# Forward and backward of a speech joint network on one core: fe rows by a transposing transfer, the first chunk's h in another tile, fewer ge loads, longer landing margins

## The chip, the cores and the metric

The kernel runs on one core of a Trainium2 chip. The metric is the device time of one execution in microseconds; lower is better. Five engines work side by side, each through its own queue in the order in which its instructions stand: TensorE (PE, its weight loads PEld), VectorE (DVE), ScalarE (ACT), GpSimd (POOL) and SyncE (SP). Here SP only issues transfers, almost all of the kernel's; they run on 16 DMA engines.

## The reference

```python
h = sum(einsum("btc,cd->btd", xp[:, i:i+T], w1[i]) for i in range(3))     # B=2, T=16000, D=256
h = gelu(h)[:, ::2]
f = sum(einsum("btc,cd->btd", hp[:, i:i+T1], w2[i]) for i in range(3))
f = gelu(f)[:, ::2]                                                       # 2 x 4000 positions
fe = einsum("btd,de->bte", f, w_f)
ge = einsum("bud,de->bue", g, w_g)                                        # U = 8
j = tanh(fe[:, :, None, :] + ge[:, None, :, :])
out = einsum("btud,dv->btuv", j, w_o)                                     # 2 x 4000 x 8 x 256
```

The kernel returns `out` and the gradients of all seven inputs for a given `grad_out`, in bf16.

## The kernel before

The 8000 positions (both batches, after the two strides of 2) are cut into 17 chunks: one of 256 positions, fifteen of 512 (four blocks of 128), one of 64. One chunk crosses from batch 0 to batch 1 (`c.mid`). Each loop step k records three stages of different chunks, so that they overlap:

- `stage_a(k+1)`: both convolutions with their gelus and gelu derivatives, then fe. `XC` is x transposed (channels on partitions), `HT` holds h (odd and even positions) and f, `FE` is fe with channels on partitions. `fe_rows` (L573) makes `FER`, fe with positions on partitions, by eight TensorE transposes (L582) into PSUM and one evacuation (`evac`, L322 on ACT or L327 on DVE). `tile_rows` (L492) makes `HR`, the rows of h and f, by one transposing transfer on SP.
- `stage_j(k)`: four steps of two u each. `JT` = tanh(fe + ge) with channels on partitions (ACT, L637); `JR`, the same with positions on partitions, from `FER` plus `GEB` (ge broadcast to all partitions) added on DVE (L660) and tanh on ACT (L665). The first two chunks (k < `NTR` = 2) have no `FER` and transpose `JT` on TensorE instead (L655). `GO_R` and `GOT` are `grad_out` as loaded and transposed. Products: `out` from JT and WO, grad w_o (`GWO`) from JR and GO_R, grad j from GOT and WOT, times 1 - tanh squared (L696, L705), summed over u into `GN` (L720).
- `stage_de(k-1)`: back through w_f, w2, w1 (`GN`, `GH` with channels on partitions), their rows `GNR` and `GHR` by transposing transfers (`grad_rows`, L759), weight gradients from HR, GNR, GHR and `XR` (rows of x), grad x through `GX_SB`.

`load_geb` (L607) loads ge's broadcast rows from DRAM (`GED`) into `GEB`, at chunk 2, at the crossing chunk and at the one after.

The order of every queue is not the order of the code. Each operation is recorded with its engine choices, an estimated cost, what it reads and writes, buffer classes with a few slots each ("ht" 1, "gh" 1, "fer" 2, "got" 3, "xc" 1 and so on), and a due time (`F.now`). `Flow.issue` (L105) then simulates the engines with these estimates and emits, one after another, the operation that can start first, with due times deciding between equals. For a transfer the model has a time to issue, a time on the one DMA ring, and a landing margin `land` after it; whoever reads the tile counts as ready only then. `ring` (L101) gives the time on the ring. So a change of `land` moves instructions on all engines without changing any of them. Nearly all matmuls are recorded through `mm` (L313), all transfers through `dma` (L337 transposing, L339 plain).

Of the kernel before, what the change touches and what calls it, by code (L numbers as in the profile page):

```python
# [35 lines left out]
class Flow:  # L36
# [5 lines left out]
    BACKLOG = {"T": 1450.0, "L": 4500.0, "S": 4500.0}  # L42
    NEAR = 300.0
    COLD = 14000.0
    KIND = 16.0

    def __init__(self, ctx, tc):
# [50 lines left out]
        self.ops.append(o)  # L98
        return o

    def ring(self, prev, kind, work):  # L101

        return work, self.TURN.get((prev or "") + kind, 0.0)

    def issue(self):  # L105
        T = {e: 0.0 for e in self.WAKE}
        avail = {e: [] for e in T}
        dma_free, dma_kind = 0.0, None
        left = len(self.ops)
        slots, seq = self.slots, self.seq  # L110

        def put(o):
            o.ready = max((d.done for d in o.deps if d not in o.soft), default=0.0)
            for e in o.eng:
                avail[e].append(o)

        for o in self.ops:
            if o.left == 0:
                put(o)
        while left:  # L120
            best = None
            for e, lst in avail.items():
                t, wake, cand, near = T[e], self.WAKE[e], None, []
                for o in lst:
                    s = o.ready + wake
                    for b in o.new:
                        st = seq[b.cls]
                        if not st[2] and st[1] != b.seq:
                            s = None
                            break  # L130
                        f = min((x[1] for x in slots[b.cls] if x[1] is not None), default=None)
                        if f is None:
                            s = None
                            break
                        s = max(s, f + wake)
                    if s is None:
                        continue
                    s = max(s, t)
                    k = (s, o.prio, o, e)
                    if e == "SP":  # L140
                        near.append(k)
                    if cand is None or k < cand:
                        cand = k
                if near:
                    lim = cand[0] + self.NEAR
                    cand = min((k for k in near if k[0] <= lim), key=lambda k: (
                        k[1][0] + (self.KIND if (k[2].xfer[0] == "T") != (dma_kind == "T") else 0.0), k[1][1]))
                if cand is not None and (best is None or cand[0] < best[0]):
                    best = cand
            assert best is not None, "no operation can start"  # L150
            s, _, o, e = best
            for x in o.eng:
                avail[x].remove(o)
            for b in o.new:
                free = [i for i, x in enumerate(slots[b.cls]) if x[1] is not None]
                i = min(free, key=lambda i: (slots[b.cls][i][1], i))
                b.slot, slots[b.cls][i][1] = i, None
                seq[b.cls][1] += 1
                b.t = slots[b.cls][i][0].tile(b.shape, b.dtype, name=b.name, tag=b.cls)
            T[e] = s + o.cost[o.eng.index(e)] * (1.8 if e == "PE" and s < self.COLD else 1.0)  # L160
            if o.xfer:
                kind, work, land = o.xfer
                if e == "SP":
                    work, gap = self.ring(dma_kind, kind, work)
# [44 lines left out]
def kernel(  # L209
# [20 lines left out]
    B, T, D = x.shape  # L230
# [130 lines left out]
    def load_xc(g_, at, apart=0.0):  # L361
# [4 lines left out]
        for n_, (b0, b1) in enumerate(cuts):  # L366
            dma("SP", lambda b0=b0, b1=b1: XC[:, b0:b1, :, :c.np].rearrange("p j k n -> p (j k) n"),
                lambda b0=b0, b1=b1: dram(xf, 4 * c.q0 - 1 + b0, 4 * c.nb, b1 - b0, c.np),
                r=[], w=[(XC, ("m", n_))], bytes_=(b1 - b0) * c.np * D * 2, new=[XC] if n_ == 0 else [], transpose=True, at=at + n_ * apart,
                land=2500.0 if c.first else 1500.0)  # L370
        if c.first:
            pool_zero(lambda: XC[:, 0, :, 0:1], [], [(XC, "z")], at=at)
            pool_copy(lambda: XC[:, 0, :, 1:P], lambda: XC[:, 4 * c.nb, :, 0:P - 1], 254, [(XC, ("m", 0))], [(XC, "h")], at=at)
# [5 lines left out]
    def load_go(g_, up, at, behind=()):  # L379
# [1 line left out]
        GO = buf("go", [P, NB, 2, V], BF16, "GO_R")  # L381
        src = gof[c.q0:c.q0 + c.W, 2 * up:2 * up + 2, :].rearrange("(p a) u v -> p a (u v)", a=c.nb)
        dma("SP", lambda: GO[:c.np, 0:c.nb].rearrange("p a u v -> p a (u v)"), lambda: src, r=[], w=[GO],
            bytes_=c.W * 1024, new=[GO], load=True, at=at, behind=behind)
        st[g_].setdefault("GO", {})[up] = GO

    def load_got(g_, up, at):
# [2 lines left out]
        GOT = buf("got", [P, NB, 2, KT, P], BF16, "GOT")  # L390
        got_op[g_, up] = dma("SP", lambda: GOT[:, 0:c.nb, :, :, :c.np].rearrange("p a j k n -> p (a j k) n"),
            lambda: GO[:c.np, 0:c.nb].rearrange("p a u v -> p (a u v)"),
            r=[GO], w=[GOT], bytes_=c.W * 1024, new=[GOT], transpose=True, at=at)
        st[g_].setdefault("GOT", {})[up] = GOT

    def load_xr(g_, at, behind=()):
# [11 lines left out]
                    r=[], w=[(XR, lo)], bytes_=(hi - lo) * nr * 512, load=True, at=at, behind=behind)  # L408
        else:
            dma("SP", lambda: flat(0, c.np), lambda: dram(xf, r0, 4 * c.nb, nr, c.np),  # L410
                r=[], w=[(XR, "m")], bytes_=c.np * nr * 512, new=[XR], load=True, at=at, behind=behind)
# [95 lines left out]
    def stage_a(g_, t0, dt):  # L507
# [2 lines left out]
        XC = S["XC"]  # L510
        nb, n_ = c.nb, c.np
        na = min(nb, 2)
        HT = buf("ht", [P, 3 * NB + 1, KT, P], BF16, "HT")
        oE, oF = nb + 1, 2 * nb + 1
        two = g_ == 1

# [38 lines left out]
        conv_gelu(g_, conv2, [hto + [W2]], HT, "f", oF, "G2", "g2", [P, NB, KT, P], None, [])  # L555
        pad_tail(g_, HT, "f", (oF, oF + nb))
        F.now = t0 + 0.48 * dt
        FE = S["FE"] = buf("fe", [P, KT, CW], BF16, "FE")
        for mt in range(KT):
            ps = psum()  # L560

# [1 line left out]
                for kt in range(KT):  # L563
                    mm(ps[:, :c.W], WF[:, kt, mt * P:(mt + 1) * P], HT[:, oF:oF + nb, kt, :n_], kt == 0, kt == KT - 1)
            op("PE", c_pe([c.W] * KT), mms, r=ftk + [WF], w=[ps], new=[ps] + ([FE] if mt == 0 else []))
            evac(lambda mt=mt: FE[:, mt, :c.W], lambda ps=ps: ps[:, :c.W], c.W, r=[ps], w=[(FE, mt)])
        F.now = t0 + 0.55 * dt
        if g_ >= NTR:
            fe_rows(g_)
        F.now = t0 + 0.75 * dt  # L570
        tile_rows(g_, "HR", "hr", HT, 3 * nb + 1, shape=[P, 3 * NB + 1, D], land=2500.0)

    def fe_rows(g_):  # L573
        c, S = chunks[g_], st[g_]
        nb, n_, FE = c.nb, c.np, S["FE"]
        FER = S["FER"] = buf("fer", [P, NB, D], BF16, "FER")
        ps = psum(BF16)

        def trs(e, ps=ps):
            for a in range(nb):  # L580
                for kt in range(KT):
                    nc.tensor.transpose(out=ps[:n_, (a * KT + kt) * P:(a * KT + kt + 1) * P],  # L582
                                        in_=FE[:, kt, a * n_:(a + 1) * n_], identity=ident[:])
        op("PE", c_pe([P] * (nb * KT)), trs, r=[FE, ident], w=[ps], new=[ps, FER])
        evac(lambda: FER[:n_, 0:nb].rearrange("p a d -> p (a d)"), lambda ps=ps: ps[:n_, 0:nb * D], nb * D,
             r=[ps], w=[FER], f=0.5)
# [18 lines left out]
            bytes_=8192, land=2500.0)  # L605

    def load_geb(c, at):  # L607
        t_ = lambda: GED[:]
        for up in range(UP):
            for lo, hi, b in parts_of(c):  # L610
                hi = P if hi == c.np else hi
                dma("SP", lambda up=up, lo=lo, hi=hi: GEB[lo:hi, 2 * up:2 * up + 2].rearrange("p u d -> p (u d)"),
                    lambda up=up, lo=lo, hi=hi, b=b: GED[b:b + 1, up * 512:(up + 1) * 512].to_broadcast([hi - lo, 512]),
                    r=[GED], w=[(GEB, up)], bytes_=(hi - lo) * 1024, load=True, at=at(up),
                    behind=[got_op[c.i - 1, 1]])

    def parts_of(c):

# [2 lines left out]
    def stage_j(g_, t0, dt):  # L621
# [2 lines left out]
        nb, n_, W = c.nb, c.np, c.W  # L624

        def cut(ap, lo, hi):
            return ap.rearrange("p (a n) -> p a n", a=nb)[:, :, lo:hi] if c.mid else ap

        def pair(up):
            F.now = tu = t0 + dt * up / UP  # L630
# [3 lines left out]
            for j in range(2):  # L634
                for mt in range(KT):
                    for k_, (lo, hi, b) in enumerate(parts_of(c)):
                        op("ACT", c_act((hi - lo) * nb, ptr=True), lambda e, j=j, mt=mt, lo=lo, hi=hi, b=b: nc.scalar.activation(  # L637
                            out=cut(JT[:, j, mt, :W], lo, hi), in_=cut(S["FE"][:, mt, :W], lo, hi), func=ACT.Tanh,
                            bias=GE[:, b, mt, 2 * up + j:2 * up + j + 1], scale=1.0),
                           r=[(S["FE"], mt), (GE, b)], w=[(JT, (j, mt, k_))],  # L640
                           new=[JT] if j == 0 and mt == 0 and k_ == 0 else [], at=tu - q * (1.0 - (2 * j + mt) / 4))
# [117 lines left out]
    def grad_rows(g_, name, cls, SRC, nblk, m):  # L759
        if chunks[g_].last:  # L760
            return pe_rows(g_, name, cls, SRC, 1, nblk, m)
        return tile_rows(g_, name, cls, SRC, nblk, lo=1, shape=[P, 2 * NB + (cls == "ghr"), D], land=3000.0)

    def stage():
        stage_n[0] += 1
# [271 lines left out]
    for b in range(B):  # L1037
# [4 lines left out]
    wload("POOL", WG, 0, lambda: WG[:], lambda: w_g.rearrange("(kt p) n -> p kt n", p=P), BIG + 1, 5000.0)  # L1042
    wload("POOL", WF, 0, lambda: WF[:], lambda: w_f.rearrange("(kt p) n -> p kt n", p=P), BIG + 2, 5000.0)
    wload("POOL", WO, 0, lambda: WO[:], lambda: w_o.rearrange("(kt p) n -> p kt n", p=P), BIG + 2, 5000.0)

    def turn(jobs, at):

# [106 lines left out]
```

## Time and profile before

| | us |
|---|---|
| median of three runs | 790.43 |
| lowest and highest of them | 787.97 and 793.09 |
| the profiled execution | 790.81 |
| its span (first to last instruction) | 789.0 |

| engine | busy us | share of the span |
|---|---|---|
| PE matmul | 769.4 | 98% |
| DVE | 719.7 | 91% |
| ACT | 711.8 | 90% |
| POOL | 83.2 | 11% |

The core moves 184.34 MB at a mean of 234 GB/s, nearly all on the SP queue. Of the groups that the change touches, the trace shows: 112 fe transposes of 128 columns on PE and two of the last chunk, 14 `FER` evacuations of 1028 ns on ACT, 16 loads of GEB, and transposing transfers `GOT` (68), `XC` (18), `HR` (17), `GNR` (16) and `GHR` (16), whose median times from issue to landing are 4.9, 9.6, 4.0, 4.4 and 7.7 us.

How to read it: a span is one execution on the profiler's clock. Matmul ends are modelled, so that PE's busy time covers the pipelining of one matmul under the next; start-to-start times say more than durations. DMA share is the mean busy share of the 16 DMA engines, and passes 1 where packets overlap on one engine. In the waits, a line says who waited for whom: total us, times, longest.

### The profile page before, as it was taken

To read this page: it belongs to the slowest core of one execution; us is meant where nothing else is said; L and a number is where in the kernel's file an instruction comes from. 1 tells how busy PE (TensorE), PEld (TensorE's weight loads), DVE (VectorE), ACT (ScalarE), POOL (GpSimd) and SP (SyncE) were. 2 spreads that over 40 slices of the span, in tenths; PEclk is the share of its full clock that TensorE was granted. 3 is DMA by queue.
4 is the path that set the end of the run, shared out by engine and by line. 5 is a ranking of instruction groups with operands and counts; after the bars stand their busy time and mean duration, and the time that the engine had idled before them with its cause. 6 is when DMAs were issued, how large, how long until landed. Compare 5 with 4: busy or idle time off the path is not lost.

```text
span 789.0 us, 15383 instructions
## 1 busy us (share of the span) xinstructions
PE 769.4 (98%) x5620; PEld 532.5 (67%) x5620; DVE 719.7 (91%) x1511; ACT 711.8 (90%) x1139; POOL 83.2 (11%) x225
## 2 busy tenths in 40 slices
PE   7899999999999999999999899999999999999997
PEld 5667667576676766767576576676757667677765
DVE  4899999998989999999999889989999899999874
ACT  4999999998899999999999799899999989999762
POOL 3011110100102010020100101002020010201000
PEclk9999999999999999999999999999999999999999
DMA  8999999999999999999999999999999999999673
GB/s 176 194 234 231 244 223 272 237 242 287 210 270 255 240 260 225 273 223 250 245 231 275 213 259 238 222 280 214 282 226 233 253 222 267 209 227 258 163 187 95
DMA packets 396052, 184.34 MB, mean 234 GB/s; under 512 B 320318, under 2 KB 389736, under 8 KB 394056
## 3 DMA queue, kind: packets, MB, share of 16 engines
q1 hardware_dynamic: 394920, 182.56, 99.6%
q8 instruction: 44, 0.72, 0.4%
q0 software_dynamic: 240, 0.41, 0.3%
q10 hardware_dynamic: 816, 0.39, 0.2%
q14 instruction: 32, 0.26, 0.1%
HBM read 52.99 MB, written 50.35 MB: 131 GB/s over the span
## 4 chain that ended last, share of the span: by engine, by line
PE 74%; ACT 8%; DVE 7%; DMA 7%; SPq 2%; issue 2%; DVEq 0%; ACTq 0%
PE ps L313 62%; PE GWO L313 10%; DMA GNR<-GN 4%; ACT JT L637 2%; ACT JSQ L696 2%; SPq L337 2%; DVE g_s L467 2%; DMA GHR<-GH 1%; DVE NGZ L705 1%; ACT JR L665 1%; ACT g_sq L463 1%; ACT HT L465 1%; PE psb L582 1%; ACT OUT_SB L322 1%; DVE ZS L720 1%
## 5 line engine op out<-in xcount | busy, mean ns | idle before, releaser
L637 ACT ACTIVATE JT<-FE,GE 128x512 bf16<-128x512 bf16 (+4 forms) x288 | 182.1, 691 | 0.0
L313 PE MATMUL ps<-GOT,WOT 128*128 128x512 bf16 (+2 forms) x544 | 150.4, 362 | 2.8 <-ACT JT L637 2.4
L705 DVE SCALAR_TENSOR_TENSOR NGZ<-JSQ,ps 128x512 f32<-128x512 bf16 (+3 forms) x252 | 151.2, 607 | 1.9 <-PE ps L313 1.7
L313 PE MATMUL ps<-WO,JT 128*128 128x256 bf16 (+1 forms) x1008 | 151.0, 273 | 0.4 <-DVE JR L327 0.3
L313 PEld LDWEIGHTS <-JT 128*128 128x128 bf16 (+1 forms) x1008 | 98.4, 98 | 62.6 <-issue 0.9
L322 ACT CAST OUT_SB<-ps 128x512 bf16<-128x512 f32 (+1 forms) x204 | 123.5, 612 | 17.2 <-PE ps L313 16.7
L696 ACT ACTIVATE JSQ<-JT 128x1024 bf16<-128x1024 bf16 (+2 forms) x126 | 129.6, 1028 | 9.7 <-DVE NGZ L705 7.6
L313 PE MATMUL GWO<-GO_R,JR 128*128 128x256 bf16 (+1 forms) x1008 | 131.0, 273 | 0.5 <-DVE JR L327 0.4
L665 ACT ACTIVATE JR<-JR 128x1024 bf16<-128x1024 bf16 (+1 forms) x116 | 123.7, 1070 | 8.2 <-DVE JR L660 8.2
L720 DVE TENSOR_TENSOR ZS<-ZS,NGZ 128x1024 f32<-128x1024 f32 (+2 forms) x102 | 115.3, 1130 | 0.7
L313 PEld LDWEIGHTS <-JR 128*128 128x128 bf16 (+1 forms) x1008 | 98.0, 98 | 16.6 <-DVE JR L327 0.7
L313 PEld LDWEIGHTS <-W 128*128 128x128 bf16 x636 | 61.0, 99 | 60.0 <-issue 2.2
L313 PE MATMUL ps<-W1T,GH 128*128 128x256 bf16 (+2 forms) x506 | 94.3, 325 | 0.0
L313 PE MATMUL ps<-GHR,XR 128*128 128x256 bf16 (+1 forms) x756 | 85.6, 273 | 0.7 <-ACT GHR L322 0.7
L313 PE MATMUL ps<-XC,W 128*128 128x512 bf16 (+2 forms) x432 | 85.8, 351 | 0.0
L313 PEld LDWEIGHTS <-XR 128*128 128x128 bf16 (+1 forms) x756 | 73.8, 98 | 9.4 <-issue 0.8
L660 DVE TENSOR_TENSOR JR<-FER,GEB 128x1024 bf16<-128x1024 bf16 (+1 forms) x116 | 77.7, 673 | 0.0
L784 DVE TENSOR_TENSOR ACC<-ACC,ps 128x512 f32<-128x512 f32 x87 | 57.8, 680 | 18.5 <-PE ps L313 18.2
L313 PEld LDWEIGHTS <-WOT 128*128 128x128 bf16 x544 | 50.6, 98 | 31.2 <-DMA GOT<-GO_R 3.3
L313 PE MATMUL ps<-GNR,HR 128*128 128x256 bf16 (+1 forms) x504 | 62.1, 273 | 6.4 <-DMA GNR<-GN 6.4
L313 PEld LDWEIGHTS <-GH 128*128 128x128 bf16 (+1 forms) x506 | 49.4, 98 | 24.6 <-issue 0.2
L463 ACT ACTIVATE g_sq<-ps 128x512 bf16<-128x512 f32 (+2 forms) x102 | 58.4, 573 | 6.8 <-PE ps L313 6.8
(131 smaller groups left out, 978.9 us busy)
## 6 DMA issues: line engine op xcount, KB each, us to landing
GO_R<-in_grad_out_dram SPq DMA_DIRECT2D x60, 512.0 KB, 5.7
out_dram<-OUT_SB SPq DMA_DIRECT2D x60, 512.0 KB, 5.2
XR<-in_x_dram SPq DMA_DIRECT2D x15, 1088.0 KB, 8.7
out_dram<-GX_SB SPq DMA_DIRECT2D x30, 512.0 KB, 5.4
out_dram<-STAGE SPq DMA_DIRECT2D x9, 128.0 KB, 1.8
GOT<-GO_R SPq DMA_TRANSPOSE x68, 4.9
GO_R<-in_grad_out_dram SPq DMA_DIRECT2D x4, 256.0 KB
out_dram<-OUT_SB SPq DMA_DIRECT2D x4, 256.0 KB
```

What stands on the lines that cost most here:

```text
L313: nc.tensor.matmul(ps_ap, lhsT=lhsT, rhs=rhs, start=start, stop=stop)
L322: nc.scalar.copy(out=dst(), in_=src())
L337: eng_.dma_start_transpose(out=out(), in_=in_())
L463: op("ACT", c_act(W, True), lambda e, mt=mt, ps=ps: nc.scalar.activation(out=sq[:, 0:nb, mt, :n_], in_=blk(ps, c), func=ACT.Square, scale= ...
L467: op("DVE", c_dve(W), lambda e, mt=mt, ps=ps: nc.vector.scalar_tensor_tensor(out=s[:, so:so + nb, mt, :n_], in0=sq[:, 0:nb, mt, :n_], scal ...
L637: op("ACT", c_act((hi - lo) * nb, ptr=True), lambda e, j=j, mt=mt, lo=lo, hi=hi, b=b: nc.scalar.activation(out=cut(JT[:, j, mt, :W], lo, h ...
L660: op("DVE", c_dve(na * 2 * D, 0.5), lambda e, h=h, na=na, JR=JR: nc.vector.tensor_tensor(out=JR[:n_, 0:na], in0=S["FER"][:n_, 2 * h:2 * h ...
L665: op("ACT", c_act(na * 2 * D), lambda e, na=na, JR=JR: nc.scalar.activation(out=JR[:n_, 0:na], in_=JR[:n_, 0:na], func=ACT.Tanh), r=[JR], ...
L696: nc.scalar.activation(out=JSQ[:, :, :W], in_=JT[:, j, :, :W], func=ACT.Square)
L705: nc.vector.scalar_tensor_tensor(out=cut(Z[:, d2, :W], lo, hi), in0=cut(JSQ[:, d2, :W], lo, hi), scalar=1.0, in1=cut(ps[:, :W], lo, hi), o ...
L720: nc.vector.tensor_tensor(out=o_, in0=i0, in1=i1, op=ALU.add)
L784: op("DVE", c_dve(512), lambda e: nc.vector.tensor_tensor(out=acc_ap().rearrange("p k d -> p (k d)"), in0=acc_ap().rearrange("p k d -> p ( ...
```

## The change

- `FE` gets the shape [128, 4, 2, 128] (block, half of the channels, position in the block) instead of [128, 2, 512]. For all chunks but the last, `fe_rows` makes `FER` from it by one transposing transfer (`tile_rows`) instead of eight TensorE transposes and an evacuation.
- The first chunk's `HT` is allocated in the buffer class of `GH` ("gh") instead of "ht", whose only slot is then not used by it.
- `load_geb` issues two loads of 1024 elements a row instead of four of 512, and in the chunk at the crossing and after it only the partitions that change batch: 6 loads instead of 16.
- The model's landing margins are longer: XC 1500 to 4500 ns (first chunk unchanged), GO, GOT and XR 1500 to 4500, HR 2500 to 4500, GNR and GHR 3000 to 8000, FER 4500, the weights WG 5000 to 8500, WF and WO 5000 to 9000. In `ring`, a transfer that starts before 10000 ns of the model's time takes 1.8 times as long.

```diff
+    CROWD = 10000.0
...
-    def ring(self, prev, kind, work):
-
-        return work, self.TURN.get((prev or "") + kind, 0.0)
+    def ring(self, prev, kind, work, free):
+
+        return work * (1.8 if free < self.CROWD else 1.0), self.TURN.get((prev or "") + kind, 0.0)
...
-                land=2500.0 if c.first else 1500.0)
+                land=2500.0 if c.first else 4500.0)
...
-            bytes_=c.W * 1024, new=[GO], load=True, at=at, behind=behind)
+            bytes_=c.W * 1024, new=[GO], land=4500.0, load=True, at=at, behind=behind)
...
-            r=[GO], w=[GOT], bytes_=c.W * 1024, new=[GOT], transpose=True, at=at)
+            r=[GO], w=[GOT], bytes_=c.W * 1024, new=[GOT], land=4500.0, transpose=True, at=at)
...
-        HT = buf("ht", [P, 3 * NB + 1, KT, P], BF16, "HT")
+        HT = buf("gh" if c.first else "ht", [P, (2 * NB + 2) if c.first else (3 * NB + 1), KT, P], BF16, "HT")
...
-        FE = S["FE"] = buf("fe", [P, KT, CW], BF16, "FE")
+        FE = S["FE"] = buf("fe", [P, NB, KT, P], BF16, "FE")
...
-            evac(lambda mt=mt: FE[:, mt, :c.W], lambda ps=ps: ps[:, :c.W], c.W, r=[ps], w=[(FE, mt)])
+            evac(lambda mt=mt: FE[:, 0:nb, mt, :n_], lambda ps=ps: blk(ps, c), c.W, r=[ps], w=[(FE, mt)])
...
-        tile_rows(g_, "HR", "hr", HT, 3 * nb + 1, shape=[P, 3 * NB + 1, D], land=2500.0)
+        tile_rows(g_, "HR", "hr", HT, 3 * nb + 1, shape=[P, 3 * NB + 1, D], land=4500.0)
...
         nb, n_, FE = c.nb, c.np, S["FE"]
+        if not c.last:
+            return tile_rows(g_, "FER", "fer", FE, nb, shape=[P, NB, D], land=4500.0)
...
-        for up in range(UP):
-            for lo, hi, b in parts_of(c):
-                hi = P if hi == c.np else hi
-                dma("SP", lambda up=up, lo=lo, hi=hi: GEB[lo:hi, 2 * up:2 * up + 2].rearrange("p u d -> p (u d)"),
+        lo, hi, b = (0, P, 0) if c.i == NTR else (c.pb, P, 1) if c.mid else (0, chunks[CB].pb, 1)
+        for h in range(UP // 2):
+            dma("SP", lambda h=h: GEB[lo:hi, 4 * h:4 * h + 4].rearrange("p u d -> p (u d)"),
...
-                            out=cut(JT[:, j, mt, :W], lo, hi), in_=cut(S["FE"][:, mt, :W], lo, hi), func=ACT.Tanh,
+                            out=cut(JT[:, j, mt, :W], lo, hi), in_=S["FE"][:, 0:nb, mt, lo:hi], func=ACT.Tanh,
...
-        return tile_rows(g_, name, cls, SRC, nblk, lo=1, shape=[P, 2 * NB + (cls == "ghr"), D], land=3000.0)
+        return tile_rows(g_, name, cls, SRC, nblk, lo=1, shape=[P, 2 * NB + (cls == "ghr"), D], land=8000.0)
```

More of the change, by code (lines that the diff above doesn't have):

```diff
@@ L163, in issue @@
                 if e == "SP":
-                    work, gap = self.ring(dma_kind, kind, work)
+                    work, gap = self.ring(dma_kind, kind, work, dma_free)
                     begin = max(dma_free + gap, s + 1300.0)
@@ L410, in load_xr @@
             dma("SP", lambda: flat(0, c.np), lambda: dram(xf, r0, 4 * c.nb, nr, c.np),
-                r=[], w=[(XR, "m")], bytes_=c.np * nr * 512, new=[XR], load=True, at=at, behind=behind)
+                r=[], w=[(XR, "m")], bytes_=c.np * nr * 512, new=[XR], land=4500.0, load=True, at=at, behind=behind)
             if c.last:
@@ L582, in trs @@
                     nc.tensor.transpose(out=ps[:n_, (a * KT + kt) * P:(a * KT + kt + 1) * P],
-                                        in_=FE[:, kt, a * n_:(a + 1) * n_], identity=ident[:])
+                                        in_=FE[:, a, kt, :n_], identity=ident[:])
         op("PE", c_pe([P] * (nb * KT)), trs, r=[FE, ident], w=[ps], new=[ps, FER])
@@ L607, in load_geb @@
     def load_geb(c, at):
-        t_ = lambda: GED[:]
-        for up in range(UP):
-            for lo, hi, b in parts_of(c):
-                hi = P if hi == c.np else hi
-                dma("SP", lambda up=up, lo=lo, hi=hi: GEB[lo:hi, 2 * up:2 * up + 2].rearrange("p u d -> p (u d)"),
-                    lambda up=up, lo=lo, hi=hi, b=b: GED[b:b + 1, up * 512:(up + 1) * 512].to_broadcast([hi - lo, 512]),
-                    r=[GED], w=[(GEB, up)], bytes_=(hi - lo) * 1024, load=True, at=at(up),
-                    behind=[got_op[c.i - 1, 1]])
+        lo, hi, b = (0, P, 0) if c.i == NTR else (c.pb, P, 1) if c.mid else (0, chunks[CB].pb, 1)
+        for h in range(UP // 2):
+            dma("SP", lambda h=h: GEB[lo:hi, 4 * h:4 * h + 4].rearrange("p u d -> p (u d)"),
+                lambda h=h: GED[b:b + 1, h * 1024:(h + 1) * 1024].to_broadcast([hi - lo, 1024]),
+                r=[GED], w=[(GEB, 2 * h), (GEB, 2 * h + 1)], bytes_=(hi - lo) * 2048, load=True, at=at(2 * h + 1),
+                behind=[got_op[c.i - 1, 1]])
     def parts_of(c):
@@ L626, in cut @@
         def cut(ap, lo, hi):
-            return ap.rearrange("p (a n) -> p a n", a=nb)[:, :, lo:hi] if c.mid else ap
+            return ap.rearrange("p (a n) -> p a n", a=nb)[:, :, lo:hi]
         def pair(up):
@@ L1041 @@
         r=[], w=[(W2, i) for i in range(KK)], bytes_=393216, load=True, at=BIG + 30.0, land=2500.0)
-    wload("POOL", WG, 0, lambda: WG[:], lambda: w_g.rearrange("(kt p) n -> p kt n", p=P), BIG + 1, 5000.0)
-    wload("POOL", WF, 0, lambda: WF[:], lambda: w_f.rearrange("(kt p) n -> p kt n", p=P), BIG + 2, 5000.0)
-    wload("POOL", WO, 0, lambda: WO[:], lambda: w_o.rearrange("(kt p) n -> p kt n", p=P), BIG + 2, 5000.0)
+    wload("POOL", WG, 0, lambda: WG[:], lambda: w_g.rearrange("(kt p) n -> p kt n", p=P), BIG + 1, 8500.0)
+    wload("POOL", WF, 0, lambda: WF[:], lambda: w_f.rearrange("(kt p) n -> p kt n", p=P), BIG + 2, 9000.0)
+    wload("POOL", WO, 0, lambda: WO[:], lambda: w_o.rearrange("(kt p) n -> p kt n", p=P), BIG + 2, 9000.0)
     def turn(jobs, at):
```

## The prediction

> **What bounds the kernel now.** I read the page first, then its groups by shape, the waits, the stretches, and the SP queue's timeline around the stalls.
>
> ```profile
> span 789.0 us, 15383 instructions
> PE 769.4 (98%) x5620; PEld 532.5 (67%) x5620; DVE 719.7 (91%) x1511; ACT 711.8 (90%) x1139; POOL 83.2 (11%) x225
> PE 74%; ACT 8%; DVE 7%; DMA 7%; SPq 2%; issue 2%; DVEq 0%; ACTq 0%
> ```
>
> TensorE carries three quarters of the chain, with VectorE and ScalarE close behind. In stretches that fit one chunk of 512 positions (columns: PE, PEld, DVE, ACT, POOL busy, clock, DMA share, GB/s):
>
> ```profile
> 165.00:212.00 47.00, 46.07 (x331) 31.79 (x330) 43.81 (x87) 41.83 (x64) 4.41 (x12) 1.00 1.06 253
> 592.20:639.60 47.40, 47.40 (x338) 32.46 (x337) 45.06 (x88) 44.89 (x69) 4.87 (x12) 1.00 1.02 239
> ```
>
> A late chunk takes 47.4 us and PE never idles in it; DVE and ACT are at 95%. So a chunk costs what its matmuls cost, as long as nothing is late. What is late, in the waits of PE:
>
> ```profile
> PE ps L313 <- DMA GNR<-GN: 6.4, 6, 3.3
> PE ps L313 <- ACT JT L637: 2.4, 1, 2.4
> PE psb L655 <- ACT JT L637: 0.7, 1, 0.7
> PE ps L313 <- DMA GOT<-GO_R: 0.4, 1, 0.4
> ```
>
> GNR, the row copy of the gradients, ends six waits; the longest has a cost behind it (PE's timeline):
>
> ```profile
> 438.08 1.05 PE L313 MATMUL ps<-GN,W2T 128*128 128x512 bf16 x8
> 442.44 1.05 PE L313 MATMUL ps<-GNR,HR 128*128 128x256 bf16 x8 [3.31 <-DMA GNR<-GN]
> 443.33 4.44 PE L313 MATMUL ps<-HT,W 128*128 128x512 bf16 x12
> ```
>
> The twelve HT,W matmuls take 4.44 us where the same twelve take 2.75 us in the chunks around: 1.7 us lost, and the granted clock of the stretch 442 to 448 is 0.72. By the Trainium skill (TensorE: Matmul & The Clock Gate, Why this matters for your kernels) an idle gap above about 3 us halves TensorE's clock for a while; the 3.31 us wait agrees, and by that rule the 1.7 us go as soon as that wait falls under 3 us, not only when it is gone.
>
> **Part 1: fe as rows by a transposing transfer.** Removed: 14 chunks times 8 transposes on PE (112 in all; the last chunk keeps its two).
>
> ```profile
> 75.25 0.45 PE psb L582 x8
> ```
>
> That is the chain's line for one such eight: 14 x 0.45 = 6.3 us of PE. Nothing else fills that time on PE, which is dense in the late chunks, so it is on the path: -6.3. Also removed are 14 evacuations of PSUM, all on ACT (FER, 1028 ns each): 14.4 us. In the built program the scheduler gives much of this back (8 GX evacuations and 3 squares move from DVE to ACT, 4 OUT_SB the other way, 2 JR to ACT); counted with each group's mean, ACT ends about 6 us and DVE about 6.5 us lower. The three engines shrink together by 0.8%, so none of them newly becomes the bound.
>
> Added: 14 transposing transfers of 256 KB on the SP queue. The nearest row has the same shape, GOT of the first chunk (128x8x128):
>
> ```profile
> 26.00 1.25 SPq L337 DMA_TRANSPOSE GOT<-GO_R  x1
> ```
>
> So SP pays 14 x 1.25 = 17.5 us, 1.25 a chunk. On the DMA engines 256 KB take 0.91 us at the page's fastest slice (287 GB/s) and 1.56 us at the rate at which a backed-up SP issues HR (852 KB in 5.06 us, 168 GB/s): 13 to 22 us in all, 0.9 to 1.6 a chunk. What hides it: SP's timeline has about 12 us of gaps in a late chunk (2.65, 3.42 and 4.22 us before single issues between 600 and 640), but only 0.5 to 2.5 us in each 47 us from 47 to 237 us, where DMA share is 1.06 to 1.09. There the cover is thin. Bounds for what reaches the end: 0, as in the late chunks, and 22 us if the queue were the bound throughout. I take 2 us, for the four chunks without gaps, half a microsecond each, nearer the low end because the bytes moved per chunk are the same early and late, while late chunks do them with 12 us to spare. It cannot be a gain by itself.
>
> Who waits for it: the vector add of FER and GEB (L660), first in DVE's order for its chunk, and behind it everything on DVE. In the built order, with matmul spacings from the chain (0.87 us for eight of 256 columns, 0.45 for eight transposes), the matmuls between fe's last one and the last result that DVE consumes ahead of that add are worth 8.2 to 20.9 us, mostly 10 to 17. GNR lands in 4.4 us (median), GHR in 7.7, and a transfer behind a full queue in 10.06 (GHR at 109.5). Two chunks at 8.2 are the tight ones; DVE could wait a microsecond or two there, and the product that needs the add stands 21 to 26 us behind fe on PE. Inside the 2 us.
>
> The new layout of FE costs nothing: tanh over split blocks already exists in the chunk that crosses the batch (352 elements 616 ns, 160 elements 458 ns), a line that gives 748 ns at 512 where the flat form takes 750. An evacuation into four blocks (HT, 616 ns) against a flat one (FE, 592): 30 x 24 ns = 0.7 us at most, hidden beside PE.
>
> **Part 2: longer landing margins.** They change no instruction, only where the consumers stand. In the two built programs, PE work between the last matmul that makes GN and the first that reads GNR grows from 8.9 us in most chunks to 13.6 to 19; the GNR products become one block of 3.4 to 3.8 us instead of being spread over 8.6. Since the waits were 3.3 us at most on top of 8.9, 4.7 more covers each: -6.4, and -1.7 for the clock. Bounds: 0 if GNR itself is later by as much (FER and the rest ahead of it in the queue), -8.1 if all go. I take -8.1, because in the chunks between 142 and 300 us GNR is also moved ahead of one or two GOT transfers that had stood before it (two took 7.76 us of SP at 147.5). Those GOTs become later: a GOT's buffer comes free 20 to 38 us of matmuls ahead of its use in most full chunks, as before, and 13.3 at the least early on, so its 4.9 us landing is covered; without that cover each would cost up to its landing.
>
> **Part 3: first chunk's h in the tile of grad h.** The only h tile is then free for the second chunk at once; the first convolution of chunk 1 (60 matmuls, 36 of them now ahead of the first transposes of tanh) no longer stands behind the first HR transfer (issued 20.77). Before, PE idled 2.4 + 0.4 us there for tanh and GOT, and 0.7 + 0.4 + 0.7 later on until 50 us, with DVE on the chain from 34 to 50 us. Bounds: -4.6 (all of it) to +1.5 (the HR issue, 1.55 us, now stands ahead of the first GOT). I take -3.0: the first two waits are filled by convolution, while the later ones belong to DVE, whose work there is unchanged.
>
> **Part 4: fewer ge loads.** 16 become 6: ten issues of about 0.6 us, 6 us off SP around three chunks, and 0.5 MB less. Beside other work, taken as 0; the bound is -0.9 (DMA GEB, 0.88 us on the chain at 335.9).
>
> **Sum.** The profiled execution took 790.81 us (span 789.0 and 1.8 around it), 0.4 above the median of 790.43. -6.3 + 2.0 - 8.1 - 3.0 = -15.4, so 775.4 for that run and 775.0 against the median.
>
> **The rivals.** (a) *The queue takes the stalls back.* Only the transposes' time is gained; the GNR waits are replaced by waits for FER, GOT or GNR in the chunks from 47 to 237 and around 332 to 427 us, where SP has no gaps. For it: DMA share above 1. Against: the distances above. Time: 790.4 - 6.3 = 784, or 781 with the start gained. (b) *Slower: DVE held by FER.* The add stands in DVE's order ahead of work that PE needs; if that holds PE up by more than (15.4 + 2)/14 = 1.25 us in every chunk, the kernel is no faster. With SP behind 6 to 8 us of XC or HR issue (8.19 at 67.2), 2.5 us a chunk would be 35 us: 775 - 2 + 35 = 808. Against: FER stands after HR, a load and a store in the late chunks, and 8 to 21 us are there. (c) *Slower: the DMA queue as the bound.* 14 x 1.56 = 22 us, no PE gain: 790 + 22 = 812. For it: the share of 1.02 to 1.09. Against: late chunks keep 12 us of SP gaps. Beside it, the Trainium skill (DMA: Bandwidth & Descriptors, Specifications) puts line rate at 512 B and more, with read-modify-write below; FER comes in pieces below that, as 320318 of the 396052 packets already do, so by that page the upper price of the transfer is the likelier and (c) gains weight. The rows' rate for such transfers (GOT, 512 KB in 1.8 to 3 us of SP) does not bear a worse price out.
>
> **How the numbers follow.** Forecast 0.68; (a) 0.20; (b) and (c) together 0.12. A median of three runs spread over 5 us tells about 1%, 7.9 us, from no change. Faster by over 1% are the forecast and a small part of (a), the one at 781: 0.70; the rest of (a) is within 1%: 0.18; slower are (b) and (c): 0.12. The likeliest case's own range is 790.4 - 6.3 - 8.1 - 4.6 - 2 (small idle times under 0.15 us, some 8 us in all) = 769 to 775 + 7 = 782. To leave out no more than 2 in 10, the range takes in (a) and a few microseconds below the sum: 766 to 787.
>
> **What would show it.** Right: no L582 rows but two for the last chunk; no GNR releaser in PE's waits above 1 us in sum; a late chunk of 46.9 us instead of 47.4; clock 1.00 throughout after the start; the first chunk's GOT products beginning with no 2.4 us wait. Wrong: DVE JR L660 waiting for DMA FER, SP without gaps in late chunks, GOT or XC among PE's releasers, a late chunk at 47.4 or longer.

## The result and the profile after

| | us |
|---|---|
| before, median of 20 runs (lowest to highest) | 791.31 (787.24 to 794.36) |
| after, median of 20 runs (lowest to highest) | 797.83 (790.79 to 803.63) |
| after against before | 1.0076, 95% interval 1.0059 to 1.0094 |
| the profiled execution of after (its span) | 795.34 (793.6) |

The kernel is 0.8% slower, 6 us, where 15.4 us less were forecast. One run of after, 803.63 us, fell into a slower state and is left out of the ratio. From the page of after: span, busy times, the chain, the SP queue.

```profile
span 793.6 us, 15172 instructions
PE 764.5 (96%) x5508; PEld 526.8 (66%) x5508; DVE 711.1 (90%) x1496; ACT 707.2 (89%) x1140; POOL 78.5 (10%) x225
q1 hardware_dynamic: 408542, 185.70, 103.2%
```

The 112 transposes are gone, VectorE and ScalarE are 8.6 and 4.6 us less busy, and the span is longer all the same: no engine became the bound, waiting did. Two stretches of one chunk each in after (columns: length, then PE, PEld, DVE, ACT, POOL busy, clock, DMA share, GB/s):

```profile
236.90:287.60 50.70, 49.27 (x334) 32.58 (x334) 44.24 (x87) 44.56 (x69) 3.65 (x13) 1.00 1.13 226
580.30:627.20 46.90, 46.90 (x330) 32.10 (x329) 44.81 (x87) 44.17 (x68) 4.92 (x12) 1.00 1.09 250
```

The late chunk takes the 46.9 us that were forecast. A chunk between 140 and 485 us takes 48 to 51 us, with about the same number of matmuls and fewer GB/s. In the waits, the forecast's two signs stand side by side: among PE's there is no line for GNR any more, but DVE waits for FER, ACT behind it for DVE, and PE for GN, VectorE's result.

```profile
DVE JR L662 <- DMA FER<-FE: 17.9, 7, 5.7
PE ps L314 <- DVE GN L722: 6.7, 4, 2.2
DVE JR L662 <- DMA GEB<-GED: 5.6, 2, 3.7
PE psb L657 <- ACT JT L639: 3.8, 3, 1.9
```

The longest of them in SP's timeline of after (an issue's length is the time that SP spent on it; that of XC in the full chunks runs from 4.8 to 9.7 us in this trace), then the same wait in the timelines of DVE, ACT and PE:

```profile
263.05 6.61 SPq L338 DMA_TRANSPOSE XC<-in_x_dram  x1
269.76 0.60 SPq L340 DMA_DIRECT2D GO_R<-in_grad_out_dram  x1
270.45 0.60 SPq L340 DMA_DIRECT2D out_dram<-OUT_SB  x1
271.17 5.47 SPq L338 DMA_TRANSPOSE GOT<-GO_R  x1
276.76 1.24 SPq L338 DMA_TRANSPOSE FER<-FE  x1
```

```profile
280.10 0.69 DVE L662 TENSOR_TENSOR JR<-FER,GEB 128x1024 bf16<-128x1024 bf16 x1 [5.65 <-DMA FER<-FE]
```

```profile
280.89 1.06 ACT L667 ACTIVATE JR<-JR 128x1024 bf16<-128x1024 bf16 x1 [4.15 <-DVE JR L662]
```

```profile
281.44 0.60 PE L314 MATMUL ps<-WO,JT 128*128 128x256 bf16 x4 [1.39 <-DVE ACC L786]
```

FE's second half was evacuated on DVE from 263.7 us, in 0.68 us, so it was there at 264.4. SP was then inside the issue of XC; FER was issued at 276.76, 12.4 us later, and landed in 3.3 us. The transfer itself is short; it stands in line. DVE's next instruction was the add, so an accumulation that PE needed waited too: PE lost 1.39 us of the 5.65.

To see where all of it went, the spacing that each kind of matmul has when nothing waits (0.056 us at 128 columns, 0.109 at 256, 0.216 at 512) was summed over the whole program: 755.5 us before, 749.2 after, 6.3 less as forecast. What TensorE's timeline shows above that sum, read at the first matmul of GN and WFT in a chunk near each time:

| kernel | 50 us | 138 us | 480 us | 715 us | end |
|---|---|---|---|---|---|
| before | 15.5 | 15.6 | 25.2 | 26.0 | 29.5 |
| after | 15.3 | 17.3 | 33.6 | 35.1 | 40.1 |
| margins, first h and GEB loads, no FER transfer (e1) | 14.8 | 15.2 | 16.3 | 16.6 | 21.5 |

So the first chunk gained nothing, and most of the loss lies between 140 and 485 us: of the 18.6 us by which after exceeds e1 in the end, 15.2 come there.

### The profile page after: what moved, and what is told of

It reads as the page before. It is cut to its first block, busy times and chain, and to the rows that moved or that the text cites. A ratio compares the mean times of both kernels' runs of the same rounds, so it can differ in the third digit from the quotient of the medians.

```text
span 793.6 us, 15172 instructions
## 1 busy us (share of the span) xinstructions
PE 764.5 (96%) x5508; PEld 526.8 (66%) x5508; DVE 711.1 (90%) x1496; ACT 707.2 (89%) x1140; POOL 78.5 (10%) x225
## 5 line engine op out<-in xcount | busy, mean ns | idle before, releaser
L639 ACT ACTIVATE JT<-FE,GE 128x512 bf16<-128x512 bf16 (+4 forms) x288 | 178.7, 679 | 0.3 <-DVE FE L328 0.2
L667 ACT ACTIVATE JR<-JR 128x1024 bf16<-128x1024 bf16 (+1 forms) x116 | 121.7, 1052 | 31.4 <-DVE JR L662 30.9
L698 ACT ACTIVATE JSQ<-JT 128x1024 bf16<-128x1024 bf16 (+2 forms) x131 | 132.0, 1008 | 13.8 <-DVE NGZ L707 11.4
L323 ACT CAST OUT_SB<-ps 128x512 bf16<-128x512 f32 (+1 forms) x199 | 117.1, 598 | 11.9 <-PE ps L314 11.5
L662 DVE TENSOR_TENSOR JR<-FER,GEB 128x1024 bf16<-128x1024 bf16 (+1 forms) x116 | 77.9, 675 | 26.2 <-DMA FER<-FE 17.9
L325 ACT ACTIVATE GX_SB<-ps 128x512 bf16<-128x512 f32 (+1 forms) x96 | 56.4, 611 | 5.8 <-PE ps L314 5.5
L466 ACT ACTIVATE HT<-ps 128x512 bf16<-128x512 f32 (+2 forms) x102 | 58.9, 579 | 0.0
```

Source lines behind the costliest of these rows:

```text
L323: nc.scalar.copy(out=dst(), in_=src())
L325: nc.scalar.activation(out=dst(), in_=src(), func=ACT.Copy, scale=scale)
L466: op("ACT", c_act(W, True), lambda e, mt=mt, ps=ps: nc.scalar.activation(out=h_buf[:, ho:ho + nb, mt, :n_], in_=blk(ps, c), func=ACT.Gelu_ ...
L662: op("DVE", c_dve(na * 2 * D, 0.5), lambda e, h=h, na=na, JR=JR: nc.vector.tensor_tensor(out=JR[:n_, 0:na], in0=S["FER"][:n_, 2 * h:2 * h ...
L667: op("ACT", c_act(na * 2 * D), lambda e, na=na, JR=JR: nc.scalar.activation(out=JR[:n_, 0:na], in_=JR[:n_, 0:na], func=ACT.Tanh), r=[JR], ...
L698: nc.scalar.activation(out=JSQ[:, :, :W], in_=JT[:, j, :, :W], func=ACT.Square)
```

## The experiments

Each is set against runs of the kernel before on the same chip in between; the intervals are about 0.3% wide on either side, 2.3 us. One ratio minus another times 790.8 us (the median of before in two of the batches) is given as us; such a difference is known less well than either ratio, to 0.002 to 0.005.

### One part undone, one part alone

Theory Q: the FER transfers fill an SP queue that had no room. Theory M, the rival: the margins' new order is the harm. e1 is the changed kernel without the transfer, e2 the kernel before with FE's new layout and the transfer, e3 the kernel before with the margins, e4 with the first chunk's h in the other tile and six GEB loads.

```diff
 e1 (after)
-        if not c.last:
-            return tile_rows(g_, "FER", "fer", FE, nb, shape=[P, NB, D], land=4500.0)
 e2 (before, with FE as [P, NB, KT, P])
+        if not c.last:
+            return tile_rows(g_, "FER", "fer", FE, nb, shape=[P, NB, D], land=4500.0)
 e3 (before): all lines with land=, CROWD and ring
 e4 (before): the line of HT, and load_geb
```

> The changed kernel with fe's rows made by TensorE transposes again; the other three parts stay. Theory Q (the 14 FER transfers load an SP queue that has no gaps from 95 to 480 us; FER lands late, DVE waits for it and PE falls back 2 to 3 us a chunk): the mid-kernel loss goes, the GNR waits stay away, 6.3 us of transposes come back: 780 to 785 us. Theory M (the longer margins reorder the queues badly, the transfer itself is harmless): slower than the changed kernel, 799 to 805.

> The kernel before with only fe's new layout and the FER transfer (margin 4500 for it), all other margins short. Q: the queue is as full as in the changed kernel, FER late and GNR late as well: 795 to 803. M: the transposes' 6.3 us are gained: 783 to 786.

> The kernel before with only the longer landing margins and the crowded-ring factor. Q: PE's 6.4 us of GNR waits and the 1.7 us at half clock go: 781 to 785. M: 797 to 803.

> The kernel before with the first chunk's h in the tile class of grad h and the six ge loads, nothing else. Both theories: small. The prediction's -3.0 us would give 788; the changed trace, whose excess over dense matmuls at 50 us is the same 15.3 as before, says 790 to 792.

| | median | ratio to before | interval |
|---|---|---|---|
| e1, all but the transfer | 783.69 | 0.9949 | 0.9932 to 0.9966 |
| e2, the transfer alone | 798.75 | 1.0131 | 1.0106 to 1.0155 |
| e3, margins alone | 784.63 | 0.9956 | 0.9935 to 0.9977 |
| e4, first h and GEB loads alone | 788.11 | 0.9998 | 0.9968 to 1.0028 |

Theory M fell: the margins gain 0.4%, and no line of e3's or e1's PE waits names GNR. The transfer alone loses 1.3%, and in e2's PE waits the wait that the margins remove is twice what it was before (6.4):

```profile
PE ps L313 <- DMA GNR<-GN: 13.9, 9, 4.1
PE ps L313 <- DMA GOT<-GO_R: 3.0, 2, 2.5
```

There the add waits for FER only 1.6 us in sum: it is the other transfers that came late. From e1 to after, the idle time of TensorE grew by 18.6 us, 1.33 for each of the 14 transfers.

### Load or reader

The next four ask whether it is the load of the transfers (theory L) or the add that waits for them (theory W). The first two are e1, instruction for instruction in its order, with one more transfer of 256 KB behind each of 14 HR transfers into a tile that nothing reads: once transposing, once as a plain copy. (The tile takes the place of ge's gradient rows and overwrites part of them, so the gradient of w_g is changed.) The third is the changed kernel with the stores of grad x cut to a quarter. The fourth is e1 with the FER transfer in the last five full chunks only; it is complete.

```diff
 x1, in x2 with dma_start and flat rows (e1)
+    EXTRA = fixed([P, NB, D], BF16, "EXTRA")
...
+        if NTR <= g_ < LAST:
+            o, issue_hr = F.ops[-1], F.ops[-1].fn
+            def both(e):
+                issue_hr(e)
+                nc.sync.dma_start_transpose(out=EXTRA[:].rearrange("p a (k d) -> p (a k) d", d=P), in_=HT[:, 0:NB].rearrange("p a k n -> p (a k n)"))
+            o.fn = both
 x3 (after)
-                    lambda lo=lo, hi=hi, flat=flat: flat(lo, hi), ...
+                    lambda lo=lo, hi=hi, flat=flat, part=part: flat(lo, hi)[:, 0:1024 * na // part], ...
 x4 (after)
-        if not c.last:
+        if 11 <= g_ < LAST:
```

> The version with fe's rows by TensorE and the longer margins (783.7 us), with every instruction in its place, plus one more 256 KB transposing transfer on SP in each of 14 chunks, right behind HR, of h's first four blocks into a tile that nobody reads. Theory L (the load on the transfer queue is the loss, whoever reads the tile): the changed kernel's idle time on TensorE exceeded this version's by 18.6 us for 14 such transfers, 1.33 us each, so 783.7 + 18.6 = 802, anything from 794 to 806 for it. PE's waits then name GNR, GOT or JT late, none of them the extra tile. Theory W (the loss is the vector add that waits for FER, first in DVE's order): 783.7 to 786, as no vector instruction waits for the new tile.

> The same, but the extra transfer is a plain copy of the same 256 KB, from one on-chip tile to the other, in 128 rows of 2 KB instead of a transpose. Theory L by bytes: as the transposing one, 794 to 806. Theory L by the transposing transfer's own cost (its small pieces): near 784 to 788, well under the transposing one. Theory W: 783.7 to 786.

> The changed kernel in its own order with FER by transfers, but the stores of grad x move only a quarter of each row (three quarters of that output are left out; first and last chunk as before), some 0.77 MB less per full chunk. Theory L: with the queue relieved of about three times what FER added, the loss between 140 and 485 us goes, and the 6.3 us of TensorE's transposes remain saved: 797 - 18 = 777 to 783. Theory W: FER still stands where it stood and DVE still waits for it: 792 to 797.

> The version of 783.7 us with the transposing transfer for fe's rows only in the last five full chunks, where SP had 10 to 12 us of gaps a chunk in the kernel before. Theory L: the cover is there, so 5 x 0.45 = 2.2 us of TensorE less and nothing given back: 781.5 (780 to 783). If the transfer costs wherever it stands (1.33 each): 783.7 - 2.2 + 6.7 = 788.

| | median | ratio to before | interval |
|---|---|---|---|
| x1, extra transposing transfers | 790.41 | 1.0001 | 0.9976 to 1.0027 |
| x2, extra plain copies | 787.19 | 0.9952 | 0.9928 to 0.9976 |
| x3, grad x stores cut | 783.07 | 0.9903 | 0.9874 to 0.9932 |
| x4, FER transfers late only | 781.55 | 0.9887 | 0.9862 to 0.9913 |

Neither theory met x1: the load costs 0.52% over e1, 4.1 us, not 18.6 and not 0. x2 is e1 within the interval (0.0003, known to 0.003, 2.3 us): in the medians the same bytes in long rows cost nothing, though the one profiled execution of x2 has a GNR wait of 2.9 us. The SP queue's line on the page shows the difference (packets, MB, their time as a share of 16 engines' span); e1, x1 and x2 in this order:

```profile
q1 hardware_dynamic: 393758, 182.03, 101.5%
```

```profile
q1 hardware_dynamic: 408542, 185.70, 103.6%
```

```profile
q1 hardware_dynamic: 395774, 185.70, 101.6%
```

With the spans (781.1, 790.7 and 787.7 us) that is 793, 819 and 800 us of packet time: 26 more for the 14 transposing transfers with 1056 packets each, 7 for the copies with 144 each. x3 took 13.7 us (0.0173) off the changed kernel with FER and its reader in place, as theory L said; the add's waits for FER fell from 17.9 to 7.3 us with it. x4 is 0.62% below e1 (4.9 us, where 2.2 were worked out, inside the two intervals): late, the transfers cost nothing. Two of its stretches with the transfers:

```profile
473.70:520.60 46.90, 46.90 (x330) 32.09 (x329) 45.50 (x88) 42.41 (x67) 5.14 (x12) 1.00 1.09 248
567.50:614.40 46.90, 46.90 (x330) 32.08 (x329) 45.23 (x88) 44.53 (x68) 5.50 (x12) 1.00 1.10 245
```

### The same order, emptied step by step

x5 and x6 keep the changed kernel's order on every engine. In x5 the add reads GEB where it read FER, so nothing waits for the transfers; in x6 they aren't issued either. x7 is complete: the changed kernel with FER's margin at 20000.

```diff
 x5 and x6 (after)
-                    in0=S["FER"][:n_, 2 * h:2 * h + na].unsqueeze(2).to_broadcast([n_, na, 2, D]),
+                    in0=GEB[:n_, 2 * h:2 * h + na].unsqueeze(2).to_broadcast([n_, na, 2, D]),
 x6 only
-            return tile_rows(g_, "FER", "fer", FE, nb, shape=[P, NB, D], land=4500.0)
+            tile_rows(g_, "FER", "fer", FE, nb, shape=[P, NB, D], land=4500.0)
+            F.ops[-1].fn = lambda e: None
+            return
 x7 (after)
-            return tile_rows(g_, "FER", "fer", FE, nb, shape=[P, NB, D], land=4500.0)
+            return tile_rows(g_, "FER", "fer", FE, nb, shape=[P, NB, D], land=20000.0)
```

> The changed kernel in its own order, all 14 FER transfers still issued, but the vector add reads the first operand from GEB's tile, which is always there, instead of FER (so fe is left out of the rows of tanh and the gradient of w_o is another one). The extra transfer without a reader cost 0.5% in the version with TensorE's transposes, 4.1 us. Theory W (most of the loss is the add's wait for FER and what stands behind it): 783.7 - 6.3 + 4.1 = 781.5, anything from 779 to 785. Theory L (the load alone) or theory S (the order that the model built with these transfers in it): 794 to 798, as the changed kernel.

> The same with the FER transfers not issued either: the changed kernel's order with neither the load nor the reader. Dense work alone gives 783.7 - 6.3 = 777.4 under theories W and L (775 to 780). Theory S (the order itself is bad): 790 or more. The difference to the kernel with unread FER transfers is the price of the load in this order: 4 us by the extra-transfer run, 15 or more under theory L.

> The changed kernel, complete, with one number changed: FER's landing margin in the issue model 20000 instead of 4500, so that the first product that needs the add stands 28 to 37 us of matmuls behind fe instead of 21 to 25, and the add stands later in DVE's order. Theory W: the wait is covered, 779 to 786. Theory L: the load is the same, 793 to 798.

| | median | ratio to before | interval |
|---|---|---|---|
| x5, transfers without a reader | 793.51 | 1.0039 | 1.0013 to 1.0065 |
| x6, neither | 782.87 | 0.9902 | 0.9865 to 0.9939 |
| x7, FER's margin 20000 | 792.53 | 1.0032 | 1.0006 to 1.0059 |

Theory W fell as the main cause: without the reader 0.37% goes, 2.9 us, and x7, whose trace has no wait for FER any more (but 3.2 us for GNR), gains the same 0.4%. The transfers themselves are 0.0137, 10.8 us. Two things stayed open: why the same load was 4.1 us in x1, and why x6 stands above 0.987, which e1 less 6.3 us would be.

### The cover, and the loads of ge's rows

x8 is e1's order without transposes, evacuations and transfer; x9 is x8 with x1's extra transfers. x10 is x6 with both operands of the add from a weight tile, so that it doesn't wait for GEB either.

```diff
 x8 (e1, and the add of x5); x9 the same on x1
              r=[ps], w=[FER], f=0.5)
+        if not c.last:
+            F.ops[-2].fn = F.ops[-1].fn = lambda e: None
 x10 (x6)
-                    in0=GEB[:n_, 2 * h:2 * h + na].unsqueeze(2).to_broadcast([n_, na, 2, D]),
-                    in1=GEB[:n_, 2 * up:2 * up + 2].unsqueeze(1).to_broadcast([n_, na, 2, D]), op=ALU.add),
+                    in0=WOT[:n_, 0:na].unsqueeze(2).to_broadcast([n_, na, 2, D]),
+                    in1=WOT[:n_, 0:2].unsqueeze(1).to_broadcast([n_, na, 2, D]), op=ALU.add),
```

> The version with fe's rows by TensorE and the longer margins (0.9949 of the kernel before), its order kept, but the 112 transposes and their evacuations not done, no transfer either, and the vector add reading GEB (fe is left out of the rows of tanh, the gradient of w_o is another one). Against the same emptied form of the changed kernel (0.9902). Theory S (part of the loss is the order that the model builds once it plans the FER transfers): this order gives the whole 6.3 us, 0.9949 - 0.0080 = 0.987, about 780.5 where before is 790.8. Theory L (the order is harmless): the same as the emptied changed kernel, 0.990, 783.

> The same as the emptied version with TensorE's order, plus the unread 256 KB transposing transfer behind HR in 14 chunks (its tile shares the space of ge's gradient rows, so the gradient of w_g is another one too). The extra transfer cost 0.0052 with the transposes on TensorE; in the changed kernel's order it cost 0.0137 without them. Theory C (TensorE's transposes gave the queue the time that covered it: 0.45 us a chunk less work, and the queue is full): 0.987 + 0.0137 = 1.000, 791. Theory S (its place in the changed order, between XC and the GOT transfers, is what costs): 0.987 + 0.0052 = 0.992, 784.5.

> The emptied form of the changed kernel (0.9902), with both operands of the vector add from a weight tile, so that it waits for neither FER nor the loads of ge's rows, which are still issued (the gradient of w_o is another one). If the later place of the six loads costs what one wait of 4.7 us on VectorE and TensorE's 3.4 us stall behind it show in that profile: 0.9902 - 0.0043 = 0.986, 780. If that wait was beside the path: 0.990, 783.

| | median | ratio to before | interval |
|---|---|---|---|
| x8, e1's order, no transposes, no transfers | 777.01 | 0.9849 | 0.9820 to 0.9878 |
| x9, the same with unread transfers | 789.55 | 1.0006 | 0.9983 to 1.0030 |
| x10, x6 without the wait for GEB | 776.50 | 0.9843 | 0.9812 to 0.9874 |

x9 is what theory C expected (1.000) and not what theory S did (0.992). x1 and x9 differ in TensorE's transposes, their evacuations and the add's operand, and take the same time (1.0001 and 1.0006). With the transfers in the queue, taking 6.3 us off TensorE is worth nothing that can be measured (0.0005, known to 0.0035, 2.8 us); without them (e1 to x8) it is worth 1.0%, 7.9 us. The transfers cost 1.57% here, 12.4 us. The same chunk in the stretches of x8 and of x9:

```profile
185.20:232.10 46.90, 46.90 (x329) 32.08 (x328) 45.06 (x87) 44.28 (x69) 5.65 (x12) 1.00 1.11 257
```

```profile
185.00:239.40 54.40, 48.99 (x330) 32.71 (x329) 45.35 (x87) 44.91 (x69) 5.18 (x13) 0.97 1.10 252
```

In x9's PE timeline the longest wait in that stretch is the one for GNR that the margins had removed:

```profile
208.14 5.10 PE L315 MATMUL ps<-GNR,HR 128*128 128x256 bf16 x32 [3.42 <-DMA GNR<-GN]
213.08 0.59 PE L315 MATMUL ps<-GOT,WOT 128*128 128x512 bf16 x2
```

The 32 matmuls take 5.10 us instead of 32 x 0.109 = 3.49. That wait and the slow matmuls behind it make 5.0 of the 7.5 us that the chunk loses, and the chunk has most of what x9 loses: above the dense sum, x9 is 11.3 us over x8 at 715 us. In the two chunks ahead of it, from 90 to 185 us, SP is without an issue for only 2.0 and 1.3 us, each holds one extra transfer near its start, and TensorE loses nothing. So the cost comes in a few long waits, and a full queue alone is not yet a loss.

x6 against x8 is the order's own share, 0.0053 or 4.2 us, and x10 is 0.0059 below x6 (both differences are known to 0.005): the wait for GEB accounts for it. In x6 it stands so on DVE, and then on PE:

```profile
425.75 0.69 DVE L664 TENSOR_TENSOR JR<-GEB 128x1024 bf16<-128x1024 bf16 x1 [4.67 <-DMA GEB<-GED]
```

```profile
428.92 0.69 PE L314 MATMUL ps<-GN,WFT 128*128 128x512 bf16 x2 [3.21 <-DVE GN L724]
429.40 1.06 PE L314 MATMUL ps<-GOT,WOT 128*128 128x512 bf16 x2
430.25 1.06 PE L314 MATMUL ps<-WO,JT 128*128 128x256 bf16 x4
```

### The sum of the steps

| step | from, to | ratio | us |
|---|---|---|---|
| margins, first h, fewer GEB loads | before, e1 | -0.0051 | -4.0 |
| no fe transposes | e1, x8 | -0.0100 | -7.9 |
| the order built with the transfers planned: wait for GEB | x8, x6 | +0.0053 | +4.2 |
| the transfers' load | x6, x5 | +0.0137 | +10.8 |
| the add that reads FER | x5, after | +0.0037 | +2.9 |
| all | before, after | +0.0076 | +6.0 |

The five steps add up to the measured ratio because they form one chain of kernels. As differences they are known to 1.3, 2.7, 3.7, 3.6 and 2.5 us in this order, so the order's 4.2 and the add's 2.9 are barely clear of nothing, while the load's 10.8 is three times its error. The best complete kernel of the study is x4, 1.1% faster than before: the margins everywhere, the transfer only where the queue has room.

## Why the prediction was wrong

The step that failed is in Part 1: "I take 2 us, for the four chunks without gaps, half a microsecond each, nearer the low end because the bytes moved per chunk are the same early and late, while late chunks do them with 12 us to spare". The price was inside its bounds of 0 and 22 us, which the runs put at 10.8 and 12.4. The low end was a choice against the row beside it: SP without gaps says that there is no cover now, whatever the queue manages later. The thin cover also reached further than the four chunks: after loses from 140 to 485 us, seven chunks, and the prediction's own rival (a) names 332 to 427 us as a stretch without gaps, which the 2 us leave out. Of the 21.4 us between forecast and result, the transfers' load and their reader make 11.7 (10.8 + 2.9 against 2.0), the wait for GEB 4.2, and the small worth of Parts 2 to 4 (4.0 against 11.1) 7.1; the transposes gave 1.6 more than forecast.

- **PE's transposes, -6.3: right as work, wrong as time.** The dense sum fell by 6.3, and alone the step is worth 7.9. With the transfers in the queue it is worth nothing that can be measured (x1 and x9), and the prediction added it and the queue's price as if one did not depend on the other. Of its rivals, (c) named that: the queue as the bound and no PE gain. It was priced at 22 us for the whole kernel, because it let the queue bind in every chunk; late ones run at 46.9 us.
- **Who waits for FER: taken as inside the 2 us.** The add waited 17.9 us in seven places, 5.7 at the longest, and it cost 2.9. The distances in matmuls (8.2 to 20.9 us) were compared with landing times of 4 to 10 us from issue. The 12.4 us from FE's end to the issue were left out of the comparison; with them FER came 15.7 us after FE.
- **Part 2, the margins: right in mechanism, too large.** The GNR waits are gone in e1, e3 and x8 (in x6, whose order is planned with the transfers, 2.9 us of them remain), and TensorE's idle time at 715 us falls from 26.0 to 18.2 in e3. By the medians it is 0.44%, 3.5 us (interval 1.8 to 5.1), not 8.1: the profiled executions differ by more than the medians do, and the sum was made on one of them.
- **Part 3, -3.0: not there.** e4 is at 0.9998 (0.9968 to 1.0028); its trace has 14.4 us of idle time at 50 us against 15.5, 1.1 less. The 2.4 us wait is gone as forecast, but two waits for GOT (1.6 and 1.4 us) came in its place. In after the sum is back at 15.3: three waits for tanh (L657, 3.8 us) stand there, and e3, which has the margins without the moved tile, has them too. The step assumed that what fills a wait shortens the stretch; yet the prediction itself had VectorE on the chain from 34 to 50 us, and the work there is unchanged.
- **Part 4, 0: right alone, wrong in the changed order.** Alone no difference; but most of the six larger loads stand later in that order (the last two are issued at 420 and 426 us in x6, at 381 and 416 in x8), which made a wait of 3.7 us in after and of 4.67 in x6: 4.2 us by x6 against x8, 4.7 by x10 against x6.
- **Rival (a)** (784, the stalls come back) had the right kind of mechanism, waits for FER, or for GNR and GOT (e2), in the chunks without gaps, but foresaw no loss beyond the gain. **Rival (b)** (808) had the add's wait at 2.5 us a chunk; it was 17.9 us in all and mostly beside the path.

Not settled: why the same transfers leave SP 3.7 to 5.0 us without an issue in each chunk of after from 532 to 674 us, and 1.4 to 2.2 from 90 to 288. The order of the queue differs early (XC stands behind GHR, not ahead of it), but no run changed only that. Nor is it shown why some chunks with a full queue lose several microseconds and others nothing.

## What to carry to other kernels

A queue without gaps in a stretch has no cover left there: what one more transfer costs is then set by who waits for the transfers behind it, not by its own length. The 14 transfers cost 10.8 and 12.4 us in sum, but in x9 the chunks from 90 to 185 us lost nothing, the next one 7.5 us, and those behind 573 us nothing again. And work taken off TensorE was worth 7.9 us without the transfers, and nothing measurable with them, so a saving on an engine and a load on the queue can't be added up as if they were independent. A swap of engine work for a transfer is to be priced chunk by chunk, and is safe where the queue has room, as in x4. When asking whether a transfer's reader waits, count from the moment when the data are there, with the time in the queue, not from the issue.

## What the runs showed of the hardware

- A transposing transfer of 256 KB costs more queue time than a plain copy of the same bytes: 1056 packets against 144, 26 against 7 us of packet time for 14, and 4.1 us against 0.2 (each known to some 2.4) in the kernel's time. The Trainium skill (DMA: Bandwidth & Descriptors, Latency and other measured facts) gives 261 GB/s for one kind of transposing transfer, and 350 to 400 where the data are contiguous. No run here shows the rate of one such transfer by itself: the 10.8 to 12.4 us are waits of the engines, not lengths of transfers.
- The DMA share doesn't tell whether a chunk loses time: 1.09 in a late chunk of after that loses nothing, 1.10 in x9's chunk of 54.4 us, 1.11 in x8's of 46.9. The issues on SP are longer where it has no gaps (XC 4.8 to 5.5 us in a late chunk of after, 6.6 to 9.7 from 95 to 475 us), but they tell no loss either: e1 has XC at 9.1 us between 91 and 137 us, and TensorE's idle time stays at 15.2 there.
- Shorter gaps than expected slow TensorE down. In after's PE timeline a wait of 2.21 us was enough:

```profile
435.95 0.60 PE L314 MATMUL ps<-GN,WFT 128*128 128x512 bf16 x2 [2.21 <-DVE GN L722]
436.39 0.87 PE L314 MATMUL ps<-GOT,WOT 128*128 128x512 bf16 x2
437.05 1.06 PE L314 MATMUL ps<-WO,JT 128*128 128x256 bf16 x4
```

The four matmuls of the last line take 0.60 us elsewhere, and the granted clock from 436 to 438 us is 0.64. In the traces of before, after and the 14 experiments, between 60 and 745 us, 17 gaps were over 2.3 us beyond a matmul's own spacing: 14 of them (2.35 to 4.24 us) were followed by half-speed matmuls, which cost 1.5 to 1.8 us each (2.9 after the longest), and three (2.36, 2.38 and 3.10) by none. Of some 30 gaps from 1.0 to 2.2 us none was. The Trainium skill (TensorE: Matmul & The Clock Gate, HAM oscillation — how this bites in real kernels) puts the limit at about 3.4 us; these runs put it near 2.3, with no sharp edge, so the prediction's sentence that the loss goes once a wait falls under 3 us does not hold.
